# Fourier mixing and a PReLU layer: tokens in groups of four rows, and the first block of 512 tokens as two of 256

## The chip, the cores and the metric

The kernel runs on one core of a Trainium2 chip. The core has five engines, each with its own instruction queue that runs strictly in order: TensorE (PE, matrix multiplication into the accumulators of PSUM), VectorE (DVE), ScalarE (ACT), GpSimd (POOL, which here only issues DMAs) and SyncE (SP, which issues the other DMAs). The metric is the time of one execution on the device, in microseconds (us). The runs of the kernel before took 777.92, 777.49 and 776.89 us, median 777.49.

## The reference

For each of 8 sequences of 3008 tokens with 256 channels, the tokens are filtered in the frequency domain along the sequence, and every token then goes through a two-layer network with a PReLU between the layers:

```python
X = np.fft.rfft(x, axis=1)                      # x: (8, 3008, 256)
Y = X * (filt_r + 1j * filt_i)[None]
y = np.fft.irfft(Y, n=3008, axis=1)
h = y.reshape(24064, 256) @ w_in                # (256, 2048)
g = np.maximum(h, 0) + alpha * np.minimum(h, 0) # alpha per column of h
out = g @ w_out                                 # (2048, 256), float32
```

## The kernel before

**The transform.** 3008 is 94 x 32: token index = 32 x + r, with x from 0 to 93 and r, the row, from 0 to 31. The transform and its inverse are done as two factors each, all as matmuls. The forward part has stages `piece_a` (94-point factor), a turn through DRAM (`save_a`, `turn_a`, for sequences 1 to 7), `piece_b` (32-point factor and the filter; the product's halves are exchanged by DMAs `sw<-ww` and added in `piece_s`) and `piece_c` (32-point factor back). After another turn (`turn_c`, then a reload into `zt`) the last 94-point factor is `inverse` (L278): for one row r, one matmul gives all 94 tokens with that r, transposed, channels on partitions. `half_d` does four rows (376 tokens) of one half of the channels, `pair_d` eight rows; each copies its result from PSUM into `yT`, the layer's input, which holds two sequences. The first sequence (class `First`) does its turns on PE: `half_t` and `piece_t` (L401, L406) multiply two or four rows by an identity into PSUM and copy them into `zt`.

**Order of tokens in `yT`.** A sequence is stored in groups of NX = 752 tokens: eight rows, and inside a group the token order is x first and then the row (x, then m of 8). `store` (L506) puts chunks of 128 tokens back in place in the output and splits a chunk that crosses the border of a group into two DMAs.

**The layer.** Tokens are done in blocks of 512 (one of 384 in each pair of sequences). A block has 16 steps, one for each slice of 128 of the 2048 hidden columns. `up(j)` (L526) does the first layer of slice j: two matmuls, 512 tokens wide, into one of two banks of an accumulator `hps` (pool `psH`, two accumulators of two banks each; `piece_a` and `piece_c` take theirs from it too). After every second slice ACT copies both banks as 16-bit into a part of `g` (`gtb`, nine buffers of four slices). DVE then makes m = (alpha - 1) min(g, 0), one instruction per slice (L543), and after four slices adds it (L545). The second layer of a block runs during the next block: `start_down` lists its 64 matmuls, and `down(q)`, one of 16 units of four, is taken from a queue `units` by `pop`. Its accumulators `op` come from pool `psO`, and ACT copies each finished pair of token chunks into `osb` for the store.

**What sets the order.** The schedule is written by hand. Steps are counted through the whole kernel; `put(step, ...)` plans a stage of a transform at a step, `put_h` also notes that it takes an accumulator of `psH`. The main loop (L657) goes through blocks and steps, calls what is planned, then `up(j)`, and takes one unit of second layer per step. In block 0 there are no units to take yet.

**The start of the layer.** The first sequence's rows 0 to 7 (group 0) are turned by four `half_t` and transformed by four `half_d` before step 0 (L491 to L495), with warm matmuls (`warm`, an identity product that nobody reads) as fillers. Groups 1 to 3 follow by plan (L615): `piece_t` at steps 0 and 3 and `pair_d` at 6 and 12 for group 1. `slopes` prepares alpha - 1 at step 1. `piece_a` of sequence 1 is planned at steps 12, 14, ... 26. For sequence 3 the turn back from DRAM, `turn_a`, is planned in two parts at steps 150 and 164 (L639):

```python
for i, (evict, kind) in enumerate(((on_act, "o"), (on_dve, "o"), (on_act, "f"), (on_dve, "h"))):
    f0.half_t(i, evict, kind)
for i, evict, kind, fill in ((0, on_act, "h", 1), (2, on_dve, "o", 0), (1, on_act, "o", 1), (3, on_dve, "f", 0)):
    f0.half_d(i, evict, kind, fill)
```

Of the kernel before, what the change touches and what calls it, by code (L numbers as in the profile page):

```python
# [14 lines left out]
N1 = 94  # L15
# [2 lines left out]
D = 256  # L18
NB = 8
DFF = 2048  # L20
NX = N1 * 8
AF = mybir.ActivationFunctionType
OP = mybir.AluOpType

# [30 lines left out]
def kernel(  # L55
# [87 lines left out]
    def banks(wide):  # L143
        if wide:
            return psH.tile([128, 2, 512], FP32, name="hps")
        return psF.tile([128, 2, 512], FP32, name="psF")
# [10 lines left out]
    class Fft:  # L157
# [127 lines left out]
        def half_d(self, i, evict, kind, fill=0):  # L285
            g, dh, mh = i // 4, (i // 2) % 2, i % 2
            pd = bank(kind)
            warm(fill, pd)
            ps = self.inverse(pd, g, dh, mh)
            t0 = self.base + g * NX  # L290
            evict(yT[:, dh, t0 : t0 + NX].rearrange("p (x m) -> p x m", m=8)[:, :, 4 * mh : 4 * mh + 4],
                  ps.rearrange("p m x -> p x m"))

        def pair_d(self, i, evict):
            g, dh = i // 2, i % 2
            ps = banks(False)
            for mh in range(2):
                self.inverse(ps[:, mh], g, dh, mh)
            t0 = self.base + g * NX
            evict(yT[:, dh, t0 : t0 + NX].rearrange("p (x h m) -> p x h m", h=2, m=4),  # L300
                  ps[:, :, 0 : 4 * N1].rearrange("p h (m x) -> p x h m", m=4))

    def on_act(o, i):
        nc.scalar.activation(o, i, AF.Copy)  # L304

    def on_dve(o, i):
        nc.vector.tensor_copy(o, i)
# [4 lines left out]
    class First(Fft):  # L312
# [85 lines left out]
                    nc.tensor.matmul(pt[0:96, u // 2, o : o + 128], m[:, 8 * f + s // 4, :, s % 4], id16,  # L398
                                     start=True, stop=True)

        def half_t(self, i, evict, kind):  # L401
            pt = bank(kind).unsqueeze(1)
            self.turn(pt, i, 2)
            evict(self.zt[:, 2 * i : 2 * i + 2].rearrange("p a d -> p (a d)"), pt[0:96, 0])

        def piece_t(self, i, evict):  # L406
            pt = banks(i == 2)
            self.turn(pt, i, 4)
            evict(self.zt[:, 4 * i : 4 * i + 4].rearrange("p (h a) d -> p h (a d)", h=2), pt[0:96])

# [78 lines left out]
    for o in (32, 96):  # L489
        nc.gpsimd.dma_start(out=filt_s[o : o + 32], in_=filt_s[o - 32 : o])  # L490
    warm(4, bank("h"))  # L491
    for i, (evict, kind) in enumerate(((on_act, "o"), (on_dve, "o"), (on_act, "f"), (on_dve, "h"))):
        f0.half_t(i, evict, kind)
    for i, evict, kind, fill in ((0, on_act, "h", 1), (2, on_dve, "o", 0), (1, on_act, "o", 1), (3, on_dve, "f", 0)):
        f0.half_d(i, evict, kind, fill)  # L495


    sizes = [512] * 5 + [384] + [512] * 6
    blocks = []
    for p in range(NB // 2):  # L500
        t = 0
        for n, tn in enumerate(sizes):
            blocks.append((p, t, tn, 2 * p + (n >= 6)))
            t += tn

    def store(p, t0, osb, lane):  # L506
        t = t0
        while t < t0 + 128:
            b, r = 2 * p + t // NFFT, t % NFFT
            g, o = r // NX, r % NX  # L510
            n = min(t0 + 128 - t, NX - o)
            row = b * NFFT + (o // 8) * N2 + 8 * g
            nc.sync.dma_start(
                out=bass.AP(tensor=out.tensor, offset=out.offset + row * D,
                            ap=[[N2 * D, n // 8], [D, 8], [1, D]]),
                in_=osb[t - t0 : t - t0 + n, lane])
            t += n

# [2 lines left out]
    class Block:  # L521
# [4 lines left out]
        def up(self, j):  # L526
            tn = self.tn
            if j % 2 == 0:
                self.hps = psH.tile([128, 2, 512], FP32, name="hps")
            for kt in range(2):  # L530
                nc.tensor.matmul(self.hps[:, j % 2, 0:tn], win_s[:, kt, j * 128 : (j + 1) * 128],  # L531
                                 yT[:, kt, self.t0 : self.t0 + tn], start=(kt == 0), stop=(kt == 1))
            if j % 2 == 1:
                i = j // 2 % 2
                if i == 0:
                    self.g = gtb[:, 2 * (gturn[0] % 9) : 2 * (gturn[0] % 9) + 2].rearrange("p a b c -> p (a b) c")
                    self.m = p_m.tile([128, 4, 512], FP16, name="m")
                    gturn[0] += 1
                g, m = (t[:, :, 0:tn] for t in (self.g, self.m))
                nc.scalar.activation(g[:, 2 * i : 2 * i + 2], self.hps[:, :, 0:tn], AF.Copy)  # L540
                for h in range(2):
                    a = alm_s[:, j - 1 + h : j + h]
                    nc.vector.tensor_scalar(m[:, 2 * i + h], g[:, 2 * i + h], 0.0, a, OP.min, OP.mult)  # L543
                if i == 1:
                    nc.vector.tensor_add(g, g, m)  # L545
                    self.gts += [g[:, h] for h in range(4)]

        def start_down(self, last):
            n = self.tn // 128
# [23 lines left out]
    def put(step, fn, *args):  # L573
        plan.setdefault(step, []).append((fn, args))
# [36 lines left out]
        nc.vector.tensor_copy(al_s, alp[:, 0:16])  # L611
        nc.vector.tensor_scalar(alm_s, al_s, 1.0, -1.0, OP.mult, OP.add)

    put(1, slopes)
    for g, ts, ds, te, de in ((1, (0, 3), (6, 12), on_act, both[::-1]), (2, (19, 23), (25, 28), on_dve, (on_dve, on_dve)),  # L615
                              (3, (32, 34), (41, 47), on_act, (on_act, on_act))):
        for i in range(2):
            put(ts[i], f0.piece_t, 2 * g + i, te)
            put(ds[i], f0.pair_d, 2 * g + i, de[i])

    def neg(ha, hb):
# [12 lines left out]
    for b in range(3, NB):  # L634
        p = 96 * (b - 1)
        if b == 3:
            a_at = (106, 112, 118, 124, 130, 132, 140, 144)
            x_at = (57, 69, 92, 98)
            ta = (150, 164)  # L639
        else:  # L640
            a_at = [p - 96 + t for t in (-34, -22, 2, 2, 14, 26, 38, 50)]
            x_at = [[p - 96 + t for t in r] for r in
                    ((-66 if b == 4 else -68, -52, -40), (-32, -18, -10), (-20, -4, 8), (4, 20, 32))]
            ta = (p - 39, p - 28)
        plan_fft(b, a_at, ta, x_at, range(p + 2, p + 74, 12), 8, range(p + 14, p + 86, 12), d_steps(p))
# [8 lines left out]
                blk.down(q)  # L654

    last = 0
    for p, t0, tn, _ in blocks:  # L657
        blk = Block(p, t0, tn)
        for j in range(16):
            n = psum.get(step, 0)  # L660
            if step < 150:
                pop(1 if n else 0)
            else:
                pop(n)
            for fn, args in plan.pop(step, ()):
                fn(*args)
            if step >= 150:
                pop(n)
            blk.up(j)
            if n:  # L670
                last = step
            else:
                soon = any(t in psum for t in range(step + 1, step + 14))
                if not (step >= 150 and step % 2 and step - last > 2 and soon and len(units) < 18 - j):
                    pop(1)
            step += 1
        blk.start_down(step == 16 * len(blocks))
        units.extend((blk, q) for q in range(16))
# [32 lines left out]
```

## Time and profile before

| | |
|---|---|
| median of the runs | 777.49 us |
| the profiled execution: its own time, its span | 777.81 us, 776.0 us |
| PE busy, share of the span | 760.5 us, 98% |
| DVE busy | 630.9 us, 81% |
| ACT busy | 587.5 us, 76% |
| POOL busy | 145.1 us, 19% |
| first matmul of the first layer | at 36.87 us |
| `piece_t` of step 32 (first matmul) | at 68.11 us |
| granted TensorE clock, mean | 1.000 |

The span runs from the first to the last instruction of the execution. A line of a group of instructions reads: line of the kernel, engine, operation, output<-input, shapes, count | busy us in all, mean ns of one | idle time of the engine just before them, and what ended it. A line of waits reads: engine, tile and line that waited <- engine, tile and line that ended the wait: us in all, times, longest. A line of the timeline has the start in us, the length in us, the engine, line, operation and count, and in brackets the idle time before it and what ended it. An engine that is not the bottleneck may idle at no cost; here it is idle time of PE that counts.

### The profile page before, as it was taken

What the parts mean: (1) busy time and instruction counts of PE and PEld (TensorE: products, weight loads), DVE (VectorE), ACT (ScalarE), POOL (GpSimd) and SP (SyncE); (2) the same over time, 40 slices, a digit from 0 to 9 for tenths busy, and PEclk for the clock granted to TensorE, in tenths of its full rate; (3) what the DMA queues carried; (4) which work ended last, traced back from release to release, by engine and by line L of the source; (5) the groups of instructions that cost most, each with busy time, mean ns of one, the idle gap of its engine ahead of it and who ended that gap; (6) DMA issues with size and microseconds to landing.
All of it is one profiled execution on the core that took longest, in us unless ns stands there. A gap on an engine that the chain in (4) does not pass through costs nothing.

```text
span 776.0 us, 16285 instructions
## 1 busy us (share of the span) xinstructions
PE 760.5 (98%) x6413; PEld 506.0 (65%) x6413; DVE 630.9 (81%) x1149; ACT 587.5 (76%) x673; POOL 145.1 (19%) x274
## 2 busy tenths in 40 slices
PE   7889999999999999999999999999999999999997
PEld 4556666666566666666666666766666666766666
DVE  3778975788888998899978999899877888666663
ACT  4787787888778777787877877787876777677663
POOL 7520661122202112112201212021110112000000
PEclk9999999999999999999999999999999999999999
DMA  9995699654764459625794438743464233511112
GB/s 169 179 234 162 104 216 218 181 118 131 163 168 105 114 130 177 182 65 121 164 200 128 100 93 181 198 103 99 130 150 111 60 81 95 150 36 28 41 41 55
DMA packets 97500, 100.53 MB, mean 130 GB/s; under 512 B 11940, under 2 KB 83764, under 8 KB 97232
## 3 DMA queue, kind: packets, MB, share of 16 engines
q1 hardware_dynamic: 82736, 70.00, 34.2%
q0 software_dynamic: 14688, 29.49, 21.3%
q8 instruction: 50, 0.82, 0.4%
q14 instruction: 26, 0.21, 0.1%
HBM read 55.52 MB, written 46.66 MB: 132 GB/s over the span
## 4 chain that ended last, share of the span: by engine, by line
PE 91%; DMA 4%; ACT 2%; POOL 1%; DVE 1%; issue 1%; DVEq 0%; ACTq 0%; POOLq 0%
PE op L562 41%; PE hps L531 41%; PE psF L281 3%; PE hps L259 2%; PE psF L228 1%; PE hps L174 1%; ACT gtb L540 1%; DMA xs<-in_x_dram 1%; PE hps L200 1%; DMA filt_s<-in_filt_r_dram 1%; DMA zt<-v_dram 1%; DMA sw<-ww 1%; DMA filt_s<-in_filt_i_dram 1%; POOL filt_s L138 0%; PE psF L398 0%
## 5 line engine op out<-in xcount | busy, mean ns | idle before, releaser
L540 ACT ACTIVATE gtb<-hps 128x1024 f16<-128x1024 f32 (+1 forms) x384 | 385.5, 1007 | 134.7 <-PE hps L531 133.7
L562 PE MATMUL op<-wout_s,gtb 128*128 128x256 f16 x3008 | 431.4, 273 | 0.0
L531 PE MATMUL hps<-yT,win_s 128*128 128x512 f16 (+1 forms) x1536 | 426.6, 375 | 1.7 <-ACT gtb L540 1.4
L562 PEld LDWEIGHTS <-gtb 128*128 128x128 f16 x3008 | 291.0, 98 | 164.4 <-issue 10.7
L543 DVE TENSOR_SCALAR m<-gtb,alm_s 128x512 f16<-128x512 f16 (+1 forms) x768 | 232.3, 346 | 104.1 <-ACT gtb L540 102.8
L545 DVE TENSOR_TENSOR gtb<-gtb,m 128x2048 f16<-128x2048 f16 (+1 forms) x192 | 231.0, 1203 | 10.5
L531 PEld LDWEIGHTS <-win_s 128*128 128x128 f16 x1536 | 145.9, 98 | 58.8 <-issue 7.7
L242 POOL DMA_DIRECT2D sw<-ww x144 | 71.6, 505 | 418.3 <-DVE ww L235 412.6
L567 ACT ACTIVATE osb<-op 128x512 f32<-128x512 f32 (+1 forms) x97 | 56.6, 583 | 12.3 <-PE op L562 11.2
L304 ACT ACTIVATE asb<-hps 128x1024 f16<-128x1024 f32 (+1 forms) x56 | 56.7, 1019 | 6.6 <-PE hps L174 5.3
L304 ACT ACTIVATE v<-hps 128x1024 f16<-128x1024 f32 (+1 forms) x43 | 43.4, 1010 | 12.3 <-PE hps L259 11.7
L235 DVE TENSOR_TENSOR ww<-psF,filts_s 128x1024 f16<-128x1024 f32 x42 | 51.2, 1218 | 0.2 <-PE psF L228 0.2
L236 DVE TENSOR_TENSOR uu<-psF,filt_s 128x1024 f16<-128x1024 f32 x42 | 51.0, 1215 | 0.0
L304 ACT ACTIVATE yT<-psF 128x752 f16<-128x752 f32 x59 | 46.9, 795 | 3.1 <-PE psF L281 3.0
L281 PEld LDWEIGHTS <-zt 96*128 96x128 f16 x512 | 28.5, 98 | 7.7 <-issue 1.0
L281 PE MATMUL psF<-wi_s,zt 96*128 96x94 f16 x500 | 31.2, 206 | 1.0 <-DMA zt<-v_dram 0.6
L247 DVE TENSOR_TENSOR uu<-uu,sw 128x1024 f16<-128x1024 f16 x36 | 24.6, 683 | 3.5 <-DMA sw<-ww 3.0
L240 POOL DMA_DIRECT2D uu<-ww x24 | 19.3, 1228 | 32.4 <-DVE uu L236 26.6
L117 POOL DMA_DIRECT2D xs<-in_x_dram x32 | 21.6, 881 | 17.7 <-PE hps L174 10.7
L184 DVE TENSOR_TENSOR xs<-xs 47x2048 f16<-47x2048 f16 x16 | 19.5, 1220 | 0.4
L188 DVE TENSOR_TENSOR xs<-xs 47x2048 f16<-47x2048 f16 x16 | 19.4, 1209 | 0.0
L259 PE MATMUL hps<-uu,twi_s 64*64 64x256 f16 x336 | 17.3, 281 | 1.6 <-DVE uu L247 1.6
(77 smaller groups left out, 226.2 us busy)
## 6 DMA issues: line engine op xcount, KB each, us to landing
out_dram<-osb SPq DMA_DIRECT2D x160, 128.0 KB
v_dram<-v SPq DMA_DIRECT2D x84, 128.0 KB
zt<-v_dram SPq DMA_DIRECT2D x28, 384.0 KB
sw<-ww POOLq DMA_DIRECT2D x144, 64.0 KB, 2.8
xs<-in_x_dram POOLq DMA_DIRECT2D x44, 192.0 KB, 6.5
at<-a_dram SPq DMA_DIRECT2D x40, 192.0 KB
a_dram<-asb SPq DMA_DIRECT2D x32, 192.0 KB
a_dram<-asb SPq DMA_DIRECT2D x12, 384.0 KB
```

The lines of the kernel that those rows point to most:

```text
L235: nc.vector.tensor_mul(ww, px, fs)
L236: nc.vector.tensor_mul(uu, px, f)
L242: nc.gpsimd.dma_start(out=sw[o : o + 32], in_=ww[i : i + 32])
L259: nc.tensor.matmul(ps[64 * par : 64 * par + 64, e, 256 * h : 256 * h + 256], twi_s[r, 4 * q + 2 * h + par], u[r, par, h], start=True, stop ...
L281: nc.tensor.matmul(ps[:, m], self.zt[:, 8 * g + 4 * mh + m, dh * 128 : dh * 128 + 128], wi3_s, start=True, stop=True)
L304: nc.scalar.activation(o, i, AF.Copy)
L531: nc.tensor.matmul(self.hps[:, j % 2, 0:tn], win_s[:, kt, j * 128 : (j + 1) * 128], yT[:, kt, self.t0 : self.t0 + tn], start=(kt == 0), st ...
L540: nc.scalar.activation(g[:, 2 * i : 2 * i + 2], self.hps[:, :, 0:tn], AF.Copy)
L543: nc.vector.tensor_scalar(m[:, 2 * i + h], g[:, 2 * i + h], 0.0, a, OP.min, OP.mult)
L545: nc.vector.tensor_add(g, g, m)
L562: nc.tensor.matmul(self.op[:, si - s0], self.gts[k][:, 128 * si : 128 * si + 128], wout_s[:, k], start=(si == s0 and k == 0), stop=(si == ...
L567: nc.scalar.activation(osb[:, 0:m], self.op[:, 0:m], AF.Copy)
```

## The change

- `NX` is 376: a group is four rows, and a sequence has eight groups. `half_d` writes one whole group as one contiguous piece, `pair_d` two groups, and `store` uses runs of four rows. The 128-token chunks of the output cross 15 borders in a pair of sequences, not 7.
- The first block of 512 tokens becomes two blocks of 256 tokens and eight steps each, so that all later blocks keep their steps. Its first layer is the new method `up4`: four slices, 256 tokens wide, fill one accumulator; one copy on ACT, four slope instructions 256 wide and one add of 4 x 256 on DVE follow. Each group of four slices takes a buffer of `g`, half filled.
- The second layer of the first half is taken from step 8 on, two units of two matmuls per step; that of the second half from step 16 on, one unit of two per step.
- Before step 0 stay `half_t(0)`, `half_t(1)` with their copies, the matmuls of `half_t(2)`, `half_t(3)`, and `half_d(0)`, `half_d(2)`. The copies of `half_t(2)`, `half_t(3)` and `slopes` go behind the matmuls of the first `up4`; `half_d(1)` and `half_d(3)` go to step 2. Two warm matmuls go away.
- Group 1's rows: `piece_t` at steps 4 (copy on ACT) and 6 (copy on DVE), both into `psF`; `pair_d` at 9 (copy on DVE) and 13 (copy on ACT).
- `turn_a` of sequence 3 at steps 146 and 165.

```diff
-NX = N1 * 8
+NX = N1 * 4
...
-            t0 = self.base + g * NX
-            evict(yT[:, dh, t0 : t0 + NX].rearrange("p (x m) -> p x m", m=8)[:, :, 4 * mh : 4 * mh + 4],
-                  ps.rearrange("p m x -> p x m"))
+            t0 = self.base + (2 * g + mh) * NX
+            evict(yT[:, dh, t0 : t0 + NX].rearrange("p (x m) -> p x m", m=4), ps.rearrange("p m x -> p x m"))
...
-            t0 = self.base + g * NX
-            evict(yT[:, dh, t0 : t0 + NX].rearrange("p (x h m) -> p x h m", h=2, m=4),
-                  ps[:, :, 0 : 4 * N1].rearrange("p h (m x) -> p x h m", m=4))
+            t0 = self.base + 2 * g * NX
+            evict(yT[:, dh, t0 : t0 + 2 * NX].rearrange("p (h x m) -> p h x m", h=2, m=4),
+                  ps[:, :, 0 : 4 * N1].rearrange("p h (m x) -> p h x m", m=4))
...
-        def half_t(self, i, evict, kind):
+        def half_t(self, i, kind):
             pt = bank(kind).unsqueeze(1)
             self.turn(pt, i, 2)
-            evict(self.zt[:, 2 * i : 2 * i + 2].rearrange("p a d -> p (a d)"), pt[0:96, 0])
+            return self.zt[:, 2 * i : 2 * i + 2].rearrange("p a d -> p (a d)"), pt[0:96, 0]
 
         def piece_t(self, i, evict):
-            pt = banks(i == 2)
+            pt = banks(False)
...
-    for i, (evict, kind) in enumerate(((on_act, "o"), (on_dve, "o"), (on_act, "f"), (on_dve, "h"))):
-        f0.half_t(i, evict, kind)
-    for i, evict, kind, fill in ((0, on_act, "h", 1), (2, on_dve, "o", 0), (1, on_act, "o", 1), (3, on_dve, "f", 0)):
-        f0.half_d(i, evict, kind, fill)
+    on_dve(*f0.half_t(0, "o"))
+    on_act(*f0.half_t(1, "o"))
+    later = [f0.half_t(2, "h"), f0.half_t(3, "f")]
+    f0.half_d(0, on_act, "o")
+    f0.half_d(2, on_dve, "o")
...
-            row = b * NFFT + (o // 8) * N2 + 8 * g
+            row = b * NFFT + (o // 4) * N2 + 4 * g
             nc.sync.dma_start(
                 out=bass.AP(tensor=out.tensor, offset=out.offset + row * D,
-                            ap=[[N2 * D, n // 8], [D, 8], [1, D]]),
+                            ap=[[N2 * D, n // 4], [D, 4], [1, D]]),
...
+        def up4(self, i, mid):
+            ps = psH.tile([128, 2, 512], FP32, name="hps").rearrange("p b (q c) -> p (b q) c", q=2)
+            for h in range(4):
+                j = 4 * i + h
+                for kt in range(2):
+                    nc.tensor.matmul(ps[:, h], win_s[:, kt, j * 128 : (j + 1) * 128],
+                                     yT[:, kt, self.t0 : self.t0 + 256], start=(kt == 0), stop=(kt == 1))
+            for fn in mid:
+                fn()
+            gg = gtb[:, 2 * (gturn[0] % 9) : 2 * (gturn[0] % 9) + 2].rearrange("p a b c -> p (a b) c")
+            g, m = (t[:, :, 0:256] for t in (gg, p_m.tile([128, 4, 512], FP16, name="m")))
+            gturn[0] += 1
+            nc.scalar.activation(g, ps, AF.Copy)
+            for h in range(4):
+                a = alm_s[:, 4 * i + h : 4 * i + h + 1]
+                nc.vector.tensor_scalar(m[:, h], g[:, h], 0.0, a, OP.min, OP.mult)
+            nc.vector.tensor_add(g, g, m)
+            self.gts += [g[:, h] for h in range(4)]
...
-    put(1, slopes)
-    for g, ts, ds, te, de in ((1, (0, 3), (6, 12), on_act, both[::-1]), (2, (19, 23), (25, 28), on_dve, (on_dve, on_dve)),
-                              (3, (32, 34), (41, 47), on_act, (on_act, on_act))):
+    put(2, f0.half_d, 1, on_act, "o")
+    put(2, f0.half_d, 3, on_dve, "o")
+    for g, ts, ds, te, de in ((1, (4, 6), (9, 13), both, both[::-1]), (2, (19, 23), (25, 28), (on_dve, on_dve), (on_dve, on_dve)),
+                              (3, (32, 34), (41, 47), (on_act, on_act), (on_act, on_act))):
         for i in range(2):
-            put(ts[i], f0.piece_t, 2 * g + i, te)
+            put(ts[i], f0.piece_t, 2 * g + i, te[i])
...
-            ta = (150, 164)
+            ta = (146, 165)
...
+    for h in range(2):
+        blk = Block(0, 256 * h, 256)
+        for j in range(8):
+            n = psum.get(step, 0)
+            pop(2 * (n > 0))
+            if j % 2 == 0:
+                blk.up4(j // 2, [] if step else [lambda: on_dve(*later[0]), lambda: on_act(*later[1]), slopes])
+            for fn, args in plan.pop(step, ()):
+                fn(*args)
+            if not n:
+                pop(2)
+            step += 1
+        blk.start_down(False)
+        units.extend((blk, q) for q in range(16))
+
+    for p, t0, tn in blocks[1:]:
```

More of the change, by code (lines that the diff above doesn't have):

```diff
@@ L502 @@
         for n, tn in enumerate(sizes):
-            blocks.append((p, t, tn, 2 * p + (n >= 6)))
+            blocks.append((p, t, tn))
             t += tn
@@ L656 @@
     last = 0
-    for p, t0, tn, _ in blocks:
+    for h in range(2):
[13 more added lines that the diff above has]
+    for p, t0, tn in blocks[1:]:
         blk = Block(p, t0, tn)
```

## The prediction

> **What bounds it now.** I read the page first: TensorE (PE) is busy 98% of the span, and the chain that ended last is 91% PE work. So a change pays only where it fills a hole of PE or takes PE work away.
>
> ```profile
> PE 760.5 (98%) x6413; PEld 506.0 (65%) x6413; DVE 630.9 (81%) x1149; ACT 587.5 (76%) x673; POOL 145.1 (19%) x274
> ```
>
> Then PE's own waits in stretches: after the start there are few, and these are the ones that the edits touch (windows 40:120 and 120:300; engine, line, releaser: total, times, longest).
>
> ```profile
> PE hps L531 <- ACT gtb L540: 1.2, 4, 0.4
> PE hps L174 <- ACT asb L304: 0.6, 1, 0.6
> PE psF L281 <- DVE yT L307: 0.2, 1, 0.2
> ...
> PE hps L259 <- DVE uu L247: 1.6, 1, 1.6
> PE psF L281 <- DMA zt<-v_dram: 0.6, 1, 0.6
> ```
>
> The timeline of PE shows the first kind in place: the first block has no second-layer work to put between its first-layer matmuls, so PE waits for ScalarE (ACT) to empty the accumulators.
>
> ```profile
> 41.44 1.94 PE L531 MATMUL hps<-yT,win_s 128*128 128x512 f16 x8 [0.39 <-ACT gtb L540]
> 43.57 1.02 PE L531 MATMUL hps<-yT,win_s 128*128 128x512 f16 x4 [0.20 <-ACT gtb L540]
> 44.76 0.49 PE L281 MATMUL psF<-wi_s,zt 96*128 96x94 f16 x8 [0.16 <-DVE yT L307]
> ...
> 48.22 1.02 PE L531 MATMUL hps<-yT,win_s 128*128 128x512 f16 x4 [0.32 <-ACT gtb L540]
> ...
> 50.41 1.02 PE L531 MATMUL hps<-yT,win_s 128*128 128x512 f16 x4 [0.30 <-ACT gtb L540]
> ```
>
> A shown idle time leaves out the pipeline's tail of some 0.2 us: the transform ahead of 41.44 starts at 40.55 and issues for 0.34, so the hole in issuing is 0.55, not 0.39. Last, VectorE (DVE) by form, since the change halves its widths.
>
> ```profile
> L545 DVE TENSOR_TENSOR gtb<-gtb,m 128x2048 f16<-128x2048 f16 x176 | 215.7, 1226 | 9.1
> L543 DVE TENSOR_SCALAR m<-gtb,alm_s 128x512 f16<-128x512 f16 x704 | 214.9, 348 | 92.6 <-ACT gtb L540 91.5
> ...
> L247 DVE TENSOR_TENSOR uu<-uu,sw 128x1024 f16<-128x1024 f16 x36 | 24.6, 683 | 3.5 <-DMA sw<-ww 3.0 <-issue 0.4
> ...
> L543 DVE TENSOR_SCALAR m<-gtb,alm_s 128x384 f16<-128x384 f16 x64 | 17.3, 316 | 11.5 <-ACT gtb L540 11.3
> ```
>
> **Part 1: the first 32 steps.** From step 32 (piece_t(6), at 68.11) the orders of PE, ACT and DVE are the same in both kernels, so the delay of that point is the price of this part. I lay the new order out from 34.94, where PE ends half_t, with durations of the trace.
>
> PE issue, by starts in the timeline: two 512-wide matmuls 0.43, eight 256-wide 0.87 (the second layer's form; a weight load of 0.098 hides under each 0.109, so half-blocks cost PE nothing extra), eight turns (piece_t) 0.68, pair_d 0.34, half_d 0.17. The same matmul columns are done, less two warm fillers of 0.22 each: -0.43. Work in this stretch: first layer of two blocks 13.9, second layer of one 6.9, piece_a 3.5, four piece_t 2.7, pair_d and half_d 2.0, slopes 0.2: 29.2, and 29.6 before. Before, 34.94 to 68.11 is 33.17, so 3.6 is holes.
>
> ACT's 1024-wide copy: 1.02 long, next start after 0.92. PE's end to ACT's start 0.2, a release 0.04. DVE: a 512-wide slope is 0.348, a 384-wide 0.316, which extrapolates to 0.284 at 256, and next start after 0.20 (0.26 at 512); the add at 1024 is L247's 0.683, next start after 0.60. A half-block group of four slices so takes 3 x 0.20 + 0.28 + 0.03 + 0.60 = 1.51 of DVE, and eight groups 12.1 where four groups took 9.2.
>
> - half_d(0) needs ACT's copy of half_t(1), 34.42 + 0.59 = 35.01: PE 35.05 (hole 0.11). half_d(0), half_d(2) to 35.39; DVE copies the second by 36.11; up4(0) starts 36.15: **hole 0.76**. Before, piece_t(2) lay here. That the first layer starts 0.7 earlier than 36.87 is thus no gain by itself.
> - up4(0), slopes, up4(1), half_d(1), half_d(3), up4(2), piece_t(2), up4(3) run to 40.81 without a hole. ACT follows: up4(0) 37.21, up4(1) 38.24, half_d(1) 39.16, up4(2) 39.53, piece_t(2) 40.45 to 41.47. piece_t(3) needs that psF bank: 41.51, **hole 0.70**. Then up4(4) to 43.05 (its tokens' last copy, half_d(3) on DVE, ends 41.83), four second-layer matmuls to 43.49.
> - pair_d(2), step 9, needs piece_t(3)'s copy, now on DVE, queued behind the groups: up4(0) from 38.27, up4(1) from 39.78, half_d(3) 41.29, up4(2) 41.74, up4(3) 43.25, the copy 44.76 + 1.22 = 45.98. PE goes on at 46.02: **hole 2.53**, and everything behind pair_d on PE's queue, first-half second layer too, waits with it.
> - From there PE has 7.2 of work to step 16 without a hole (28 second-layer matmuls 3.04, three up4 2.6, two piece_a 0.87, two pair_d 0.68): 53.2. Before, step 16 came at 49.1 with no second layer done; these 32 matmuls are 3.5 of PE.
> - Steps 16 to 27 now hold half as much second layer. Per two steps PE has 0.87 + 0.43 (piece_a) + 0.43 = 1.73, but piece_a and the first layer share two accumulators, so one pair of slices follows the last after 0.87 + 0.20 + 1.02 + 0.04 = 2.13 (48.22 to 50.41 was 2.19). Before, 0.43 more of second layer covered this. Holes: 0.67 at step 16, 0.59 at 18, four of 0.40 to step 26: **2.84**.
>
> Holes 6.94 against 3.6, less 0.43: piece_t(6) at 71.05, **+2.9**. Bounds: with a DVE group at half its 512-wide price (2.31 / 2) the copy ends 44.8 and this is +1.8; with slopes that cost at 256 what they cost at 512, a group takes 1.76, the copy ends 47.0 and it is +3.9. I keep 2.9: the 384-wide row lies between.
>
> **Part 2: SP's queue.** Stores go from 54 to 62 per pair of sequences (15 inner group borders in 47 chunks, not 7), 32 in all at about 0.6 of SP. SP waits 367.8 us for osb, so nearly all is hidden. One is not: before piece_c's last save (122.63) SP issued two stores back to back, now three, and the reload zt<-v_dram ends in PE's wait at 133.07. Between 0 (SP waited for v anyway) and +0.7 I take **+0.5**, since 122.63 follows the store's end by 0.1.
>
> turn_a of batch 3 goes from step 150 to 146, past turn_c on SP. PE's wait at 198.6 (1.56, with the tail 1.76) is for piece_s of sw copies issued at 191.3, beside turn_a from 191.17. Sw copies, issue to landing (windows 160:175, beside v_dram writes, then 190:195, beside turn_a):
>
> ```profile
> DMA to landing us min/median/max: 1.9/2.5/2.9
> ```
> ```profile
> DMA to landing us min/median/max: 3.7/3.8/5.0
> ```
>
> A save issued at 64.25 released its turn_a at 67.39; so the save of 186.89 lets turn_a go at 190.0, 1.2 earlier, with turn_c's 512 KB behind it beside the sw copies. Full relief is -1.76, none is 0; turn_a's 768 KB still overlap, so I take the middle, **-0.8**. Step 164 to 165 meets no PE wait: 0.
>
> The Trainium skill, "DMA: Bandwidth & Descriptors", section "Queues, rings and completion order", says that each DMA engine takes turns between queues packet by packet. By that, which SP transfer is in the way would not matter while SP's queue is full, the relief would be 0 and the sum +3.4; the two rows above speak against it.
>
> **Rest.** The two zt copies put inside up4(0) run on DVE at 36.0 to 36.7 and on ACT at 35.8 to 36.4, while PE does up4(0); if they were late, up4(1) would wait as long. Block 0 takes eight of the nine g buffers, not four; the next block's second group needs the first half's second layer done, which is at step 15, four steps ahead of that group. On SP the first half's two stores now stand ahead of save_a(1) of batch 1: osb is ready near 55.0, the save's data near 57.7, so nothing waits. Its turn_a follows the last save (68.0) by the 3.1 seen before, so at 71.1, and four issues (1.9) and a landing of about 2 end near 75.0; piece_b(0) comes at 71.05 + 4.93 = 76.0, with 1.0 to spare, and a later landing would cost its excess. yT's new order keeps shape and count of the copies (752 elements, ACT 0.795); the last 128-token chunks cross no border, so the tail stands: 0.
>
> **Sum.** 2.9 + 0.5 - 0.8 = +2.6 on a profiled execution of 777.81 (span 776.0), which lies 0.3 above the median of 777.49: **780.2** against that median.
>
> **Rivals.**
> 1. *The turn_a move pays in full* (not slower). Place: 198.6; price -1.76, and no SP loss at 133. Then 2.9 - 1.8 = +1.2: 778.7, inside 0.2% (1.55 us, about what can be told from no change). It decides if sw lands in 2.9 as beside v_dram; against it, turn_a's bytes still flow then. 0.17.
> 2. *DVE is not late.* If piece_t(3)'s copy came before 43.5 the 2.53 would go: +0.4 in part 1, 777.6 with part 2. It takes DVE groups of under 0.9, where the add alone is 0.68, and ACT hands up4(3) over only at 42.4. With rival 1 on top 776.1, still within 0.2%. For a real gain something that this layout doesn't know must help: 0.08 in all.
> 3. *PE is slower after the hole.* At half clock through all 7.2 of work that follows, at most +7.2: 787. The granted clock was 1.00 in the slices after the hole at 198.6, so 0.04. The Trainium skill, "TensorE: Matmul & The Clock Gate", section "What's actually happening", has the half rate follow an idle window of about 3.4 us; my longest hole is shorter, and no run here shows one that long.
>
> **Chances.** Forecast as laid out 0.71, rival 1 0.17, rival 2 0.08, rival 3 0.04. Slower is the forecast and rival 3, 0.75; within 0.2% rival 1, 0.17; faster 0.08. Low end 776.8: most of rival 2 lies beneath; high end 782.8: upper bound of part 1 (+3.9), no relief, SP +0.7, and a little for holes that I missed; rival 3 lies outside.
>
> **What would show it.** Right: piece_t(6) near 71; one PE wait of about 2.3 for DVE's zt copy near 46; half a dozen PE waits of 0.2 to 0.4 for ACT between 53 and 68; slopes at 256 near 0.28, adds near 0.69; the PE wait at 198.6 (then near 202) under 1.5; the one at 133 near 1.1. Wrong: pair_d(2) released by ACT or with no wait, PE closed up between 53 and 68, or new DMA waits later than 75.

## The result, and the profile after

The kernel became slower: 785.50 us as the median of six executions (782.01 to 788.75) against 777.69 for the kernel before (776.89 to 777.99, six executions on the same chip), a ratio of 1.0098 with a 95% interval of 1.0070 to 1.0126. The direction was forecast, the size was not: +2.7 was forecast against the median that the forecast used, +7.8 was measured, above the range's upper end of 782.8. The profiled execution took 785.85 (span 784.1), 8.1 more in the span than the one before (776.0). Its mean granted clock is 0.995, where the one before has 1.000. In the six executions of the changed kernel that mean lies between 0.993 and 0.998. One execution of the kernel before in the later sessions, of 798.30 us at a clock of 0.949, is left out of all figures.

The page of the changed kernel: TensorE (PE) has the same matmul columns to do, less two warm matmuls, but its busy time has grown by 3.4 us.

```profile
PE 763.9 (97%) x6443; PEld 510.6 (65%) x6443; DVE 634.3 (81%) x1170; ACT 586.2 (75%) x672; POOL 145.1 (19%) x274
```

PE's own waits in the windows 40:55, 55:80, 120:160 and 200:240 (engine, line, releaser: total us, times, longest us):

```profile
PE psF L281 <- DVE zt L306: 2.3, 1, 2.3
PE psF L397 <- ACT zt L303: 0.5, 1, 0.5
...
PE hps L530 <- ACT gtb L539: 1.3, 5, 0.3
PE psF L397 <- DVE yT L306: 0.7, 1, 0.7
PE hps L530 <- ACT asb L303: 0.3, 1, 0.3
...
PE psF L281 <- DMA zt<-v_dram: 2.4, 1, 2.4
...
PE hps L259 <- DVE uu L247: 1.1, 1, 1.1
```

A shown wait leaves out a tail of about 0.2 each. With it, the first two are the holes of 2.53 and 0.70 that the prediction had laid out, and the six waits of L530 for ACT (1.3 + 0.3, and six tails) are the 2.84 of steps 16 to 26. The 0.7 for a copy to yT was not foreseen. The wait for the reload of zt was 0.6 before and was to become 1.1. It is 2.4. The last was 1.6 before.

The timeline of PE (start, duration, instruction, in brackets the idle time before it and its releaser) puts them in place:

```profile
45.69 0.49 PE L281 MATMUL psF<-wi_s,zt 96*128 96x94 f16 x8 [2.33 <-DVE zt L306]
...
46.76 1.91 PE L552 MATMUL hps<-yT,win_s 128*128 128x256 f16 x8
...
73.33 0.84 PE L397 MATMUL psF<-id,v 128*96 128x128 f16 x8 [0.72 <-DVE yT L306]
...
140.11 0.51 PE L281 MATMUL psF<-wi_s,zt 96*128 96x94 f16 x8 [2.44 <-DMA zt<-v_dram]
```

PE goes on at 45.69 (46.02 was forecast; this execution is 0.3 ahead of the one before when half_t ends). But then eight matmuls of L552 take 1.91, where the same eight take 1.04 elsewhere (at 41.88, for one). The stretches of 1 us show why. Columns: stretch, us, busy us and instructions of PE, of its weight loads, DVE, ACT and POOL, then PE's granted clock, DMA share, GB/s. The first row and the last two cover 3.41 us each, the length of one stretch of half clock: the 3.41 just ahead of the first such stretch, those just ahead of the second, and the second itself.

```profile
42.72:46.13 3.41, 1.08 (x16) 0.85 (x14) 3.38 (x10) 1.02 (x1) 0.53 (x1) 1.00 1.15 248
...
46.00:47.00 1.00, 1.00 (x11) 0.72 (x8) 0.97 (x4) 0.00 (x0) 0.00 (x0) 0.56 0.94 197
47.00:48.00 1.00, 1.00 (x6) 0.71 (x5) 0.99 (x2) 0.00 (x0) 0.00 (x0) 0.50 0.96 197
48.00:49.00 1.00, 1.00 (x7) 0.70 (x5) 0.00 (x0) 0.30 (x1) 0.00 (x0) 0.50 1.00 221
49.00:50.00 1.00, 1.00 (x9) 0.76 (x8) 0.24 (x2) 0.73 (x1) 0.00 (x0) 0.73 1.06 234
50.00:51.00 1.00, 1.00 (x12) 0.90 (x10) 0.96 (x5) 0.00 (x0) 0.23 (x1) 1.00 0.91 184
...
138.29:141.70 3.41, 1.47 (x19) 1.13 (x20) 0.37 (x2) 0.80 (x1) 0.00 (x0) 1.00 0.83 207
141.70:145.11 3.41, 3.41 (x20) 2.00 (x17) 1.30 (x3) 2.10 (x3) 0.00 (x0) 0.50 0.95 312
```

Behind each of the two long holes PE runs at half clock for some 3.4 us and does half the work in it: 0.44 + 0.50 + 0.50 + 0.27 = 1.7 us lost behind the first, and 1.6, by the lag below, behind the second.

To see where the 8.1 came from, I set the starts of the same PE instructions in both traces against each other. From half_t (it starts at 33.54 in the kernel before) to step 32 the changed kernel falls back by 5.5. From there to the reload of zt the lag stands still, at that reload it grows by 3.4, at the wait near 199 it shrinks by 0.4, and from there to the last stage it does not move. With the 0.3 by which this execution was early at half_t: -0.3 + 5.5 + 3.4 - 0.4 = 8.2.

DVE's new forms (busy total, mean ns of one, idle time before) cost what the prediction took for them, 284 and 683:

```profile
L562 DVE TENSOR_SCALAR m<-gtb,alm_s 128x256 f16<-128x256 f16 x32 | 7.0, 281 | 4.3 <-ACT gtb L559 4.3
L563 DVE TENSOR_TENSOR gtb<-gtb,m 128x1024 f16<-128x1024 f16 x8 | 5.5, 693 | 0.3
```

### The profile page after: what moved, and what is told of

Read it like the earlier page. It is cut to its first block, busy times and chain, and to the rows that moved or that the text cites. A ratio compares the mean times of both kernels' runs of the same rounds, so it can differ in the third digit from the quotient of the medians.

```text
span 784.1 us, 16397 instructions
## 1 busy us (share of the span) xinstructions
PE 763.9 (97%) x6443; PEld 510.6 (65%) x6443; DVE 634.3 (81%) x1170; ACT 586.2 (75%) x672; POOL 145.1 (19%) x274
## 4 chain that ended last, share of the span: by engine, by line
PE 89%; DMA 4%; ACT 3%; DVE 2%; POOL 1%; issue 1%; SPq 0%; DVEq 0%; POOLq 0%; ACTq 0%
PE op L580 40%; PE hps L530 39%; PE psF L281 3%; PE hps L259 2%; PE psF L228 1%; ACT gtb L539 1%; DMA xs<-in_x_dram 1%; PE hps L174 1%; PE hps L200 1%; DMA filt_s<-in_filt_r_dram 1%; ACT asb L303 1%; DMA v_dram<-v 1%; DMA filt_s<-in_filt_i_dram 1%; DMA sw<-ww 1%; POOL filt_s L138 0%
## 5 line engine op out<-in xcount | busy, mean ns | idle before, releaser
L539 ACT ACTIVATE gtb<-hps 128x1024 f16<-128x1024 f32 (+1 forms) x376 | 377.5, 1007 | 135.8 <-PE hps L530 134.2
L530 PE MATMUL hps<-yT,win_s 128*128 128x512 f16 (+1 forms) x1504 | 419.2, 375 | 2.1 <-ACT gtb L539 1.4
L542 DVE TENSOR_SCALAR m<-gtb,alm_s 128x512 f16<-128x512 f16 (+1 forms) x752 | 227.2, 345 | 103.3 <-ACT gtb L539 102.0
L544 DVE TENSOR_TENSOR gtb<-gtb,m 128x2048 f16<-128x2048 f16 (+1 forms) x188 | 226.1, 1203 | 11.1 <-DVE m L542 0.9
L530 PEld LDWEIGHTS <-win_s 128*128 128x128 f16 x1504 | 143.2, 98 | 56.5 <-issue 7.8
```

## The experiments

Three questions were open: whether the half clock is the holes' doing, why the reload of zt came 1.8 later and not 0.5, and what each part of the change costs alone. Two theories stand behind the runs. By the first, the lost time is long holes plus the half clock behind them. By its rival, PE lost only the idle time, and the rest lies in the DMA queues. Changes in the lag below are counted from half_t on, since the start before it, where the code of all fourteen kernels is alike, ends anywhere from 32.6 to 34.2 us (at 35.9 in ax_layout, which lost its clock there), and "the lag" is always against the profile of the kernel before. Ratios are against the kernel before in the same session.

### a_layout: the eight groups of four rows alone

The kernel before, with only the new token order and its stores:

```diff
-NX = N1 * 8
+NX = N1 * 4
...
-            t0 = self.base + g * NX
+            t0 = self.base + (2 * g + mh) * NX
...
```

> The kernel before with the groups of four rows alone (layout of yT and the split stores), the start and turn_a as before. Theory: the extra store ahead of the v_dram writes makes PE's wait for zt<-v_dram (0.62 at 133) longer, to between 1.0 and 2.4, with a half-clock stretch (1.7) behind it only if it passes 2; nothing else moves: 778.3 to 781.5. Rival: the stores are hidden and the longer wait comes from the later start of the layer: 777.7, the wait stays near 0.6.

Measured: 781.51 (779.09 to 782.75, ten executions), ratio 1.0041 [1.0022, 1.0059]. Nothing is lost before step 32; at the reload of zt PE waits 2.6 and then runs at half clock, and the lag grows by 3.5 there. The stretch behind that wait:

```profile
136.00:140.00 4.00, 4.00 (x25) 2.49 (x23) 1.51 (x3) 2.25 (x4) 0.00 (x0) 0.62 0.81 272
```

So the layout alone makes the second loss of the changed kernel, clock and all, with nothing of the two half-blocks. The three executions with a mean clock of 1.000 took 779.1, 779.1 and 780.4, the seven others, at 0.995 to 0.998, 781.2 to 782.8.

### b_act: the late copy moved from DVE to ACT

The changed kernel, with piece_t(3)'s copy (and piece_t(2)'s, as before) on ACT:

```diff
-    for g, ts, ds, te, de in ((1, (4, 6), (9, 13), both, both[::-1]), ...
+    for g, ts, ds, te, de in ((1, (4, 6), (9, 13), (on_act, on_act), both[::-1]), ...
```

> The changed kernel with piece_t(3)'s copy on ACT, not DVE. Theory: the PE wait of 2.33 for DVE's zt copy goes, and with it the half-clock stretch behind it (1.7): 785.5 - 4.0 = 781.5 (780.5 to 782.5), granted clock 1.00 until 70. Rival: the wait only changes its releaser, since ACT is as full as DVE there: 784 to 786.

Measured: 782.41 (779.77 to 785.92, ten), ratio 1.0060 [1.0038, 1.0081]. The hole is gone: pair_d(2) starts without a wait, between two groups of the second layer.

```profile
43.49 0.60 PE L580 MATMUL op<-wout_s,gtb 128*128 128x256 f16 x4
43.92 0.50 PE L281 MATMUL psF<-wi_s,zt 96*128 96x94 f16 x8
```

The first 32 steps now cost +1.4, not +5.5, and no half clock follows. The hole of 2.53 was thus DVE's doing, as laid out: with it went 4.1 us, of which 1.7 was clock. The wait for zt (2.2) and its half clock remain.

### c_warm and wx_warm: the holes left in place, PE kept busy

Ten matmuls with the identity, which nothing needs, are put ahead of pair_d(2), in c_warm also at step 94, ahead of the reload's users. If half clock comes from idleness, it must go, while the hole stays.

```diff
+    for at in (9, 94):
+        put(at, lambda: warm(10, bank("h")))
```

> The changed kernel with ten identity products that nobody reads (2.17 us of PE) ahead of pair_d at step 9 and at step 94, inside the two long holes; all waits stay, only PE is not idle in them. Theory (the half clock follows from PE idling about 2.5 us): granted clock 1.00 in all slices, two stretches of 1.7 saved, 785.5 - 3.4 = 782.1 (781.0 to 783.0). Rival (the clock falls for another reason, or the products only come on top): 785.5 or later.

Measured: 785.52 (783.76 to 786.24, four), ratio 1.0096 [1.0065, 1.0128]. In the first part the expectation held. PE is held to 46.45, for the same copy, and the clock stays at 1.00:

```profile
43.97 2.32 PE L427 MATMUL hps<-id 128*128 128x512 f16 x10
46.45 0.49 PE L281 MATMUL psF<-wi_s,zt 96*128 96x94 f16 x8 [0.16 <-DVE zt L306]
```
```profile
44.00:48.00 4.00, 3.84 (x32) 2.37 (x30) 3.93 (x11) 0.82 (x1) 0.00 (x0) 1.00 1.12 240
```

Steps 0 to 31 cost +3.8 instead of +5.5: the 1.7 of half clock, and nothing else. The time did not follow. The reload of zt landed 1.2 later than in the changed kernel, PE waited 1.5 for it on top of the fillers, and the wait near 199 was 2.1 (1.1 in the changed kernel). Why these DMAs were later with the fillers, no run settles.

The second form has the fillers at step 9 only, on top of x_load (below), which has no wait at the reload.

```diff
+    put(9, lambda: warm(10, bank("h")))
```

> x_load with ten identity products in the hole at step 9. Theory (the half clock comes from an idle stretch, by chance of where it falls): the waits stay, granted clock 0.999 or more in all executions, 780.0 (779.3 to 780.8), no execution over 781.5; x_load gave 779.99 to 782.43 with clocks of 0.998 to 1.000. Rival (the clock falls without regard to that hole): spread and clocks as in x_load, 781.2.

Measured: 782.66 (780.70 to 785.75, ten), ratio 1.0052 [1.0033, 1.0071], no better than x_load's 1.0049. The clock is 1.00 from 44 to 52 again and steps 0 to 31 cost +3.85, but near 200 the sw copies land later than in x_load (5.8 at most after their issue against 4.6), PE waits 2.4 there, and half clock comes with that wait (a granted clock of 0.82 from 200 to 204 and of 0.75 from 204 to 208).

So the expectation on the time fell a second time, and for the same open reason. One thing near 200 does differ in the traces: a transfer of 16 KB on the instruction queue (q8 of the page). Counted with each kernel's lag taken off, it starts at 194.5 and 194.8 in the two kernels with fillers, while the sw copies issued at 191.3 to 192.8 are still under way, and at 196.6 to 197.0 in the seven other kernels that have the half-blocks. Whether it delays the copies no run tests, and it says nothing of the reload. What the two runs show of the clock is that the hole of step 9, filled with useless matmuls, was followed by no half clock. That alone proves little, since x_load and g_turnc (below) have the same hole unfilled and no half clock either; of the three unfilled holes of step 9, one was followed by it.

### x_load: one load of x moved away from the writes of v_dram

The timeline of the DMA queue of SP (start, duration of the issues, transfer, count), before and after, around the reload of zt:

```profile
121.33 1.21 SPq L513 DMA_DIRECT2D out_dram<-osb  x2
122.63 2.60 SPq L270 DMA_DIRECT2D v_dram<-v  x4
127.91 2.43 SPq L276 DMA_DIRECT2D zt<-v_dram  x4
```
```profile
126.55 2.36 SPq L512 DMA_DIRECT2D out_dram<-osb  x3
129.01 2.17 SPq L270 DMA_DIRECT2D v_dram<-v  x4
136.32 2.48 SPq L276 DMA_DIRECT2D zt<-v_dram  x4
```

and of POOL's, first of the kernel before, then of the changed one:

```profile
125.38 1.04 POOL L117 DMA_DIRECT2D xs<-in_x_dram  x2 [5.20 <-PE hps L174]
```
```profile
130.60 1.04 POOL L117 DMA_DIRECT2D xs<-in_x_dram  x2 [5.20 <-PE hps L174]
```

The third store pushes the four writes of v_dram 1.2 later (129.01 less the lag of 5.2 is 123.8, against 122.63), and there the prediction stopped. But before, the last write was issued by 122.63 + 2.60 = 125.23, when POOL's load of x (376 KB) was only coming. After, the writes run to 131.18 and the load comes at 130.60, into them. From the end of the writes' issue to the first reload, which waits for the last write to land, it took 127.91 - 125.23 = 2.7 before and 136.32 - 131.18 = 5.1 after. The experiment leaves the third store and moves the load of x nine steps on:

```diff
-            x_at = (57, 69, 92, 98)
+            x_at = (57, 69, 92, 107)
```

> The changed kernel, stores as they are, but the fourth x load of sequence 3 planned behind the sw copies of step 106, so that it is not in flight beside the v_dram writes. Theory (contention with that load is most of the delay): the writes still start at 3.3, but land in 2.6 and not in 5.2; zt loads near 8, PE's zt wait 0.5 to 1.2 and no half clock behind it: 782.1 to 783.3. Rival (the late start alone, or another transfer): zt loads after 9.5, wait over 2, 785.

Measured: 781.15 (779.99 to 782.43, four), ratio 1.0049 [1.0032, 1.0066]. The writes are as late as in the changed kernel, but land at once, and PE no longer waits for zt:

```profile
127.38 2.25 SPq L270 DMA_DIRECT2D v_dram<-v  x4
131.66 1.73 SPq L276 DMA_DIRECT2D zt<-v_dram  x4
```

The last write was issued by 127.38 + 2.25 = 129.63, and 131.66 - 129.63 = 2.0. The lag, +3.4 there in the changed kernel, changes by -0.8. The median is under the 782.1 to 783.3 that were expected, since these had a half clock at step 9 in them. The hole of step 9 is there with 2.32, and no half clock follows (the last rows below hold two stretches of 3.41 us, both at a clock of 1.00):

```profile
45.71 0.49 PE L281 MATMUL psF<-wi_s,zt 96*128 96x94 f16 x8 [2.32 <-DVE zt L306]
```
```profile
41.70:45.11 3.41, 1.69 (x17) 1.39 (x16) 3.34 (x10) 1.42 (x2) 1.58 (x3) 1.00 1.10 226
45.11:48.53 3.42, 2.82 (x31) 2.57 (x31) 2.87 (x7) 0.98 (x1) 0.00 (x0) 1.00 1.06 225
```

So steps 0 to 31 cost +3.85 here, which is the same as with the fillers.

### ax_layout: the groups of four rows, with the moved load

The same move of the load, on a_layout. If the collision is all that the layout costs, nothing is left.

```diff
-            x_at = (57, 69, 92, 98)
+            x_at = (57, 69, 92, 107)
```

> a_layout with the fourth x load of sequence 3 planned behind step 106. Theory (the eight groups cost only through that load): the zt wait of 2.6 and the half clock behind it go, -0.7 at step 94 against the kernel before, +0.5 at the wait near 198: 777.4 (776.6 to 778.2). Rival (the split stores cost by themselves): 779 to 781.

Measured: 777.48 (776.83 to 782.02, ten), ratio 0.9993 [0.9976, 1.0010], where a_layout had 1.0041. No wait for zt is left. The new layout and its eight extra stores cost nothing that can be told, but for the collision that they set off. The profiled execution was the slowest of the ten (782.02). It had half clock at its start and again behind a wait of 1.9 near 200, the shortest that it followed from step 0 on. At the start no single wait was that long: the longest in the 3.4 us ahead of the half clock was 1.3, and PE was busy for 54% of them.

### g_turnc and best1: the writes put ahead of the stores

The last four writes of v_dram of sequence 1 and their reload go ahead of the stores of steps 79 and 80 on SP's queue, in g_turnc on the changed kernel:

```diff
     def store(p, t0, osb, lane):
+        if step in (79, 80):
+            held.append((p, t0, osb, lane))
...
-                put(c_at[q] + 1, f.turn_c, q // 2)
+                put(c_at[q] + (b > 1 or q < 5), f.turn_c, q // 2)
...
+            if step == 80:
+                while held:
+                    store_now(*held.pop(0))
```

> The changed kernel, with turn_c's last four v_dram writes of sequence 1 (and the zt loads) ahead of the three stores on SP, not behind them. In a_layout and the changed kernel those writes start 3.3 us after piece_c's start, land beside the x load that POOL issues at 4.9, and the zt loads are issued at 10.5; in the kernel before 2.1 and 7.4. Theory (the split store pushes the writes into the x load): writes near 1.6, zt loads at 7 or earlier, PE's zt wait under 0.7, no half clock near 142: 785.5 - 3.4 = 782.1 (781.0 to 783.3). Rival (the x load, not the order on SP, decides): zt loads still near 10, 785.

Measured: 784.33 (780.29 to 785.05, four), ratio 1.0079 [1.0055, 1.0103]. The profiled execution, the fastest, has no wait for zt, the hole of 2.33 at step 9, and a clock of 1.000 throughout. The median is above the 781.0 to 783.3 that were expected: the other three took 784.2 to 785.1 at clocks of 0.995 to 0.998. They left no trace, so it stays open behind which holes they lost it.

The same edit with turn_a at 146 and 165, on the kernel before:

> The kernel before with turn_a of sequence 3 at 146 and 165 and with the last v_dram writes of sequence 1 ahead of the stores on SP; layout and start as before. Theory: the zt wait at 133 (0.62) and part of the wait at 198 (1.56 to 0.9) go: 777.7 - 1.4 = 776.3 (775.6 to 777.2). Rival (both waits are made by DMA contention that only moves): 777.4 to 778.

Measured: 777.33 (775.81 to 778.72, twelve), ratio 0.9994 [0.9983, 1.0005]. The two waits fell from 0.6 to 0.2 and from 1.6 to 0.9, and the profile is 1.1 ahead from half_t on, but the time doesn't tell it from no change.

### h_ta: turn_a earlier, alone

The kernel before, with the one line:

```diff
-            ta = (150, 164)
+            ta = (146, 165)
```

> The kernel before with turn_a of sequence 3 at steps 146 and 165 alone. Theory: PE's wait for piece_s near 198 falls from 1.56 to about 1.1, as in the changed kernel: 777.7 - 0.5 = 777.2 (776.0 to 777.5). Rival (SP's transfers share the DMA engines whatever their order): 777.7, the wait stays 1.5.

Measured: 777.41 (775.93 to 778.16, ten), ratio 0.9993 [0.9976, 1.0010]. The wait at 198.6 fell from 1.6 to 0.9; the wait for zt, which the edit doesn't touch, was 1.1 in this execution. The relief is 0.6, and it is too small for the time to show.

### f_late, fx_late and bx_act: what the early second layer costs

f_late is b_act with no second layer in steps 8 to 15 and two units of it per step in 16 to 31, where the changed kernel has one:

```diff
             n = psum.get(step, 0)
-            pop(2 * (n > 0))
             if j % 2 == 0:
...
-            if not n:
-                pop(2)
             step += 1
...
+            k = 2 if step < 32 else 1
             if step < 150:
-                pop(1 if n else 0)
+                pop(k if n else 0)
```

> b_act (the changed kernel with piece_t(3) copied on ACT), but no second layer in steps 8 to 15: all of block 0's is taken in steps 16 to 31, two units of two matmuls per step. Theory (the early second layer only moves holes: what it fills in steps 8 to 15 opens again in steps 16 to 31, where two accumulators cannot go faster than 2.13 per two steps): PE at step 32 within 1.0 of b_act, which lies 1.8 behind the kernel before; median 781.4 to 783.4; the five PE waits for ACT between 55 and 70 gone. Rival (the early second layer is gain): step 32 comes 3.5 later than in b_act, 785.9.

Measured: 780.94 (779.67 to 782.36, four), ratio 1.0046 [1.0028, 1.0064]. The early second layer does more than move holes, as both the theory and the rival missed: steps 0 to 31 cost +0.2 where b_act's cost +1.4, and between 55 and 80 PE has no wait left, neither the five for ACT nor the one for yT. So both come from steps 16 to 31 being thinned. The wait for zt is 2.5, this time at a clock of 1.00, and it costs 1.9.

fx_late adds the moved load of x (the line of x_load):

> All suspects undone but the eight groups, the half-blocks and turn_a at 146/165: piece_t(3) copied on ACT, no second layer in steps 8 to 15, the fourth x load of sequence 3 behind step 106. Theory (three causes add up: the DVE copy, the early second layer, the v_dram writes beside the x load): from half_t PE is +0.2 at step 32 (as f_late), -0.6 at step 94 (as x_load against its step 32), -1.1 after the wait near 198; median 776.6 (775.9 to 777.6), the kernel before being at 777.6. Rival (something else in the eight groups costs time): 778.5 or more.

Measured: **776.72** (775.70 to 780.42, twelve), ratio 0.9980 [0.9963, 0.9997] against 778.22: the one version whose interval lies below the kernel before, by a little, and in the session in which that kernel was slowest (its medians in the other three are 777.29 to 777.79). The lag changes by +0.2 to step 32, by -0.8 at the reload of zt and by -0.4 near 199, as the parts had promised. PE's waits between 40 and 240, the first two:

```profile
PE hps L259 <- DVE uu L247: 1.2, 1, 1.2
PE psF L281 <- DVE yT L306: 0.7, 1, 0.7
```

No hole is longer than 1.2, and none is for the reload of zt. bx_act takes f_late's edit back out of fx_late, so that it is the changed kernel with two edits: the copy on ACT, the load of x moved.

> fx_late with the second layer of the first half taken eight steps on again, as in the changed kernel (so: the changed kernel with piece_t(3) copied on ACT and the late x load). Theory (the early second layer costs by itself, through the holes it leaves in steps 16 to 31): from half_t PE is 1.4 behind the kernel before at step 32, where fx_late is 0.2 behind, and +0.1 at the end: the time of the kernel before, ratio 1.000 (0.998 to 1.002), 1.2 us over fx_late. Rival (b_act and f_late differed by chance): as fx_late, ratio 0.998.

Measured: 778.16 (777.07 to 780.84, twelve), ratio 1.0015 [1.0003, 1.0027]. Its lag grows by 1.4 to step 32 and falls by 0.7 after it. With the hole of step 9 and the collision gone, the changed kernel is nearly back at the kernel before, and what keeps it behind is the early second layer: +1.4 against fx_late's +0.2 in those steps.

## Why the prediction was right in sign and wrong in size

**Part 1, the forecast +2.9: the layout held.** The hole of 2.53 stands where it was laid out, ended by the engine that was named (DVE, behind the groups); b_act removes it by removing that one cause. The 0.70 for piece_t(3) and the holes of steps 16 to 26 came as well. Even the end of the layout holds: 71.05, less 0.3 for the early start and plus 1.7 of clock, is 72.45, and there PE is done with step 31 (its last two matmuls of the second layer start at 72.23 and issue for 0.22). But piece_t(6) starts at 73.33. With the clock at 1.00 the first 32 steps cost +3.8 (c_warm, x_load and wx_warm: 3.83, 3.85, 3.85): the forecast and this one hole of 0.9.

**The step "from step 32 the orders are the same in both kernels, so the delay of that point is the price of this part" overlooked the state in which step 32 is entered.** piece_t(6) needs the psF bank that pair_d(5) filled in step 28, and DVE, with the first layer closed up by the thinned second layer, copies it only from 72.34 to 73.27; PE goes on at 73.33. f_late, with the second layer back in steps 16 to 31, has no such wait. I had followed DVE up to the last hole that I was pricing, and not up to the first instruction behind the part.

**The step that put the half clock at 0.04 failed: rival 3 is what happened, at less than its full price.** The argument was that the clock was 1.00 behind the hole of 1.56 at 198.6, and that the longest new hole was shorter than the idle window that the prediction had from the Trainium skill. The hole of 1.56 was too short a row to speak for one of 2.5. In the fourteen profiles there are, from step 0 on, eleven waits of PE between 1.9 and 2.6, and half clock follows six of them; it follows none of 1.6 or less. And it is no property of the place: behind the same hole of 2.3 at step 9 the changed kernel lost its clock and x_load and g_turnc did not.

What differs is how the hole falls on a grid in time. By the clock records of the traces, the half-clock stretches of one execution start whole multiples of 3.413 us apart: 46.13 and 141.70 in the changed kernel (28.00 windows), 24.26 and 201.75 in ax_layout (52.00). The grid lies elsewhere in each execution. With each of the fourteen traces cut into the windows of its own grid, from its first full clock on, half clock follows every window in which PE was busy for less than 40%, and none in which it was busy for more than 55%. Between them it went both ways: 0.43, 0.45 and 0.54 were followed by it, 0.42, 0.50 and 0.54 were not, the last being the window around the hole of 1.56 at 198.6. In the changed kernel the hole of step 9 lay inside one window (42.72 to 46.13, busy for 1.08, which is 32%); in x_load a border at 45.11 split it (1.69, which is 50%, and 2.82), in g_turnc one at 44.92 (56% in the emptier window). So that the profiled execution lost its clock at step 9 was luck; that a hole of this length can lose it was not.

Where it comes, it lasts about 3.4 us and costs 1.7, not the 7.2 that rival 3 gave as its bound. In the profile of the changed kernel it came twice, 3.3 us in all, the largest single term of the error; the second time it was behind the hole of part 2, where no rival looked for it (its window, 138.29 to 141.70, was busy for 1.47, which is 43%). The Trainium skill, "TensorE: Matmul & The Clock Gate", section "What's actually happening", has the clock judged in free-running windows of about 3.4 us and back at full rate after one busy window. The trace agrees: the stretches last 3.41 us, and their grid of 3.413 us runs on without regard to the kernel. What I had drawn from the Trainium skill there, that a hole must be longer than the window, the runs contradict.

**Part 2, the forecast +0.5, measured +1.8 of waiting and 1.6 of clock.** The step that failed is "before piece_c's last save SP issued two stores back to back, now three": the third store pushed the writes by 1.2, where about 0.6 had been reckoned for a store, but above all the push was taken as the whole price, with the landing of the writes unchanged. The writes' delay moved them into a load of x on POOL's queue, and their landing went from 2.7 to 5.1. The range's lower and upper ends, 0 and +0.7, both assumed that landing. x_load and ax_layout show it: with the load elsewhere and the store in place the wait is gone, and the layout's ratio falls from 1.0041 to 0.9993.

**turn_a, the forecast -0.8, measured -0.4** (1.56 to 1.1; 0.6 in h_ta). Rival 1, relief in full, is refuted. The value lies between no relief and the one taken. By the rule that the prediction quoted from the Trainium skill, "DMA: Bandwidth & Descriptors", section "Queues, rings and completion order", I had worked out no relief at all; nine of the eleven kernels with turn_a at 146 gained 0.3 to 0.65 there, and only the two with fillers lost (0.6 and 0.8).

**The sum.** The terms of the forecast give 777.49 + 2.6 = 780.1 for the median; the 780.2 on record is 0.1 more. Of the 5.5 us (5.6 with the roundings) between the forecast of +2.6 and the 8.1 of the spans, 3.3 is the clock (1.7 and 1.6), 1.3 the collision at the reload, 0.9 the hole at step 32, 0.4 the smaller relief, and -0.3 the earlier start. Without the clock the same execution would have come out near 782.5, inside the range, but still with 2.2 us, the collision and the hole at step 32, that the forecast had not seen.

## What to carry to other kernels

When a change opens a hole of some 2 us on a busy PE, price the hole and, beside it, about half a chance (six of eleven here) of a further 1.7 us at half clock behind it; a cheap copy moved to another engine can close the hole and save both. When one queue's transfers are delayed by a microsecond, don't stop at that microsecond: look at which transfers of the other queues they now meet, since that meeting here cost twice the delay, and moving the other transfer cost nothing. Taking the same work out of a later stretch to fill an earlier one is not neutral if the later stretch used it as cover for its own accumulators.

## What the runs showed of the hardware that I had not expected

- PE went to half clock after idle times of only 1.9 to 2.6 us, in six of eleven cases, for about 3.4 us each. In the fourteen traces it went by how long PE had been busy in the window of 3.413 us just ended: under 40% always cost the clock, over 55% never did. The executions that left no trace fit that: the changed kernel's six took from 782.0 us at a mean clock of 0.998 to 788.8 at 0.993, and behind them all may be one to three such stretches. The same step shows in the kernel before. Of its 87 executions in the four sessions of the experiments, 63 had a mean clock of 0.999 or more and a median of 777.45, and 24 had 0.998 or less and a median of 779.85. Where in the kernel those 24 lost it, no trace shows.
- How long four writes of 128 KB took to land, from the end of their issue, went by when one load of 376 KB on another queue was issued: 5.0 to 5.8 us with the load issued in among them (five kernels: after, a_layout, b_act, c_warm, f_late), 2.6 to 2.7 with it issued 0.1 to 0.9 us behind the last of them (before, h_ta, best1, g_turnc), and 2.0 to 2.2 with it moved away (x_load, ax_layout, wx_warm, fx_late, bx_act).
- With ten useless matmuls at step 9 the sw copies near 200, a hundred and fifty microseconds later, landed about 1 us later in both kernels that had them. The cause is open.
